# Third window's dilated pairs with v stationary, later token blocks of 256 and 320, and another model of VectorE beside GpSimd in the list schedule

## The chip, the cores and the metric

One core of one Trainium2 chip. The metric is device time in microseconds (us) of one execution; of several runs the median counts. Engines are TensorE (PE, with its weight loads PEld), VectorE (DVE), ScalarE (ACT), GpSimd (POOL) and SyncE (SP), which issues most DMAs.

## The reference

```python
# q, k, v: (4, 8, 576, 64); heads 0-3: window of 32; heads 4-7: dilated, 32 keys at a step of 4
scores = where(mask, q @ k.T / 8, -1e9)
attn = exp(scores - max(scores)); attn /= sum(attn) + 1e-9
x = (attn @ v) as (2304 tokens, 512)
h = x @ w_in;  x = maximum(0.01 * h, h) @ w_out                       # first MLP, 512 -> 2048 -> 512
h = x @ w_in2; out = (maximum(h, 0) + log1p(exp(-abs(h)))) @ w_out2   # second MLP
```

## The kernel before, in words

The 2304 tokens are cut in two ways. For attention there are eight **windows** w of 288 tokens (half a sequence each), and in each of them four **pairs** p of heads: p = 0, 1 are plain, p = 2, 3 dilated. For the first MLP there are **blocks** of tokens (`widths`, L448), and each block runs over 16 pieces f of the hidden size. One (block, f) is a **slot**. In a slot TensorE runs twelve matmuls `h<-xh,w` / `h<-xl,w` (g1, L833) and, two slots later, twelve `yp<-gh,w` / `yp<-gl,w` (g2, L876); between them ScalarE copies h out of PSUM (`hc`, L849) and rounds it (`gh`, L854), and VectorE takes the rest (`gl`, g1_lo, L858). Every operand is split into a high and a low part, so each product is three matmuls. Blocks 0 and 1 are done together, f by f, as slots 0 to 31; block 2 is slots 32 to 47, block 3 slots 48 to 63, and so on to slot 127. A block's x lies in a room of one of two buffers (`x0`, `x1`, in turn by unit; a unit is a block, blocks 0 and 1 together being unit 0), so attention for one block runs beside the slots of the block before it, and its small matmuls stand between the slots on TensorE.

A pair of attention goes: transposes of k and q (trans_k, trans_q), scores (`sc`, L661 or L674), mask (L682, L689), the maximum over keys with a PARTITION_ALL_REDUCE on GpSimd (`mx<-s`, L699), less_max (L703), exp on ScalarE, and then one of two ways. **Not turned**: pv (L724) has the probabilities stationary and v, with a column of ones for the sum, moving; ScalarE and VectorE divide (inv, L740, L741); xT (L750) transposes on TensorE; x_hi (L807) and x_lo (L811) split x. **Turned**: pv_late (L760) has v stationary, so that its result needs no transpose; the sum over keys is a second PARTITION_ALL_REDUCE (`sm<-s`, L768); VectorE spreads it (L776), inverts it (recip, L781 to L784) and multiplies (norm, L788). Windows 0 and 1 (`early`) have code of their own. Before, window 2 is not turned at all, of window 3 pairs 0, 2 and 3 are, from window 4 on all are.

Beside all this the weights of both MLPs are converted from their 64-bit form by ScalarE and VectorE (cp, cf, w: L326, L330, L339, L366, L381), and those of the second one stored in HBM as sums. From about 500 us on the second MLP runs (L1017, L1078, L1090), which the change leaves alone.

The order of every engine is found while the kernel is built: `run_schedule` (L108) is a list scheduler. Each `Op` has a cost, a due time worked back from its users' targets, slots that it acquires and releases, and the engines take the most urgent op that is ready. The order that results is fixed: on the chip each engine runs its own instructions in that order, and semaphores hold one that comes too early. For VectorE beside a reduce of GpSimd the scheduler has a model: before, an op with `lock` set runs at a share of its speed (0.33, or 0.7 for the transposes and recip) as long as the reduce lasts.

Of the kernel before, what the change touches and what calls it, by code (L numbers as in the profile page):

```python
# [11 lines left out]
F32 = mybir.dt.float32  # L12
# [14 lines left out]
def kernel(  # L27
# [22 lines left out]
    P = 128  # L50
# [4 lines left out]
    TG = 384  # L55
# [30 lines left out]
    TURN = 3  # L86
# [7 lines left out]
    class Op:  # L94
        def __init__(self, eng, cost, fn, *args, deps=(), order=(), acq=(), rel=(),
                     target=None, margin=0.0, start=0.0, lib=None, slack=0.0, lock=0.0, optional=False, hold=0.0, lead=None, shy=False):
# [11 lines left out]
    def run_schedule(slots):  # L108
# [64 lines left out]
        running = {}  # L173

        def slowed(start, work, rate):
            beside = locked - start
            return start + (work / rate if work <= rate * beside else beside + work - rate * beside)

# [5 lines left out]
        while True:  # L184
# [17 lines left out]
            for e in engines:  # L202
# [3 lines left out]
                for o in pools[e]:  # L206
                    if ready_at[o] <= now + 1e-9 and all(free[a] >= o.acq.count(a) for a in o.acq):
                        rank = (ready_at[o] if e == "bw" else o.prio) + (HOLD if switch(o) else 0.0) + (WAIT if 0.0 < o.lock < 0.5 and now < locked else 0.0), o.n
                        if best is None or rank < best_rank:
                            best, best_rank = o, rank  # L210
# [24 lines left out]
                if best.lib == "reduce":  # L235
                    locked = best.end if now > LOCK_FROM else now + LOCKED
                    beside = running.get("dve")
                    if now > LOCK_FROM and beside is not None and beside.lock and beside.end > now:
                        beside.end = slowed(now, beside.end - now, beside.lock)
                        busy["dve"] = beside.end - TRAIL["dve"]  # L240
                        heapq.heappush(events, beside.end)
                        heapq.heappush(events, busy["dve"])
# [205 lines left out]
    widths = [256, 256, 352, 288, 288, 288, 288, 288]  # L448
# [22 lines left out]

    xparts, rows = {}, {}
# [12 lines left out]
    class Pair:  # L485
        def __init__(self, w, p):
# [8 lines left out]
            self.turned = w >= TURN and (self.dil or p == 0 or w > TURN)  # L495
# [294 lines left out]
        def x_views(self):  # L790

            w0 = self.w * T1
            for u in range(NUNIT):
# [3 lines left out]
                xh, xl = (t[:, self.p, lo - unit_at[u]:hi - unit_at[u]] for t in x_room(u))  # L797
# [5 lines left out]
                yield src, xh, xl  # L803

        def x_hi(self):
            for src, hi, _ in self.x_views():
                nc.scalar.activation(out=hi, in_=src, func=AF.Copy)  # L807

        def x_lo(self):
            for src, hi, lo in self.x_views():  # L810
                nc.vector.tensor_sub(out=lo, in0=src, in1=hi.bitcast(F32))  # L811
# [326 lines left out]
    NSPIN, LOCKED, LOCK, LOCK_FROM, SLACK0, SLACK, HOLDS = 150, 1.2, 0.33, 75.0, 0.3, 1.0, 1.5  # L1138
    LOCKT = 0.7
# [53 lines left out]
    for w in range(NW):  # L1193
        blocks = [b for b, (t, n) in enumerate(BLOCKS) if t < (w + 1) * T1 and t + n > w * T1]
        first_slot = min(slot(b) for b in blocks)
        rooms = sorted({unit_of[b] for b in blocks if BLOCKS[b][0] >= w * T1 and b != 1})
        for p in range(NPAIR):
# [58 lines left out]
            else:  # L1256
                nk = a.s0 + T1 - a.klo
                tk = Op("dve", dve(nk) if not dil or a.first else 2 * dve(nk), a.trans_k, deps=[lk] + old_kq, rel=["kr"], lock=LOCKT, **m)
                tq = [Op("dve", (1.0 if turned else 1.2) if dil else 0.48, a.trans_q, deps=[lq] + (old_kq if dil else []),
                         rel=["qr"] if dil else [], lock=LOCKT, **m)]  # L1260
# [25 lines left out]
            x = Op("dve", dve(576), a.less_max, deps=[r], rel=[tag_mx], lock=LOCK, **m)  # L1286
            a.o_less = x
            x = [Op("act", act(576), a.exp, deps=[x], **m)]
            if turned:
# [3 lines left out]
                t = Op("dve", 2 * dve(288), a.spread, deps=[sm, pv], rel=[tag_mx, tag_s], lock=LOCKT, **m)  # L1293
                t = Op("dve", 0.9, a.recip, deps=[t], acq=["rd"], rel=["rd"], lock=LOCKT, **m)
# [17 lines left out]
            xh = a.o_xh = Op("act", act(288, not turned), a.x_hi, deps=[xt], order=[prev(1, "o_xh")],  # L1312
# [316 lines left out]
```

## Time and profile before

| | |
|---|---|
| median of 3 runs (lowest to highest) | 892.06 us (892.01 to 892.25) |
| profiled execution, own time | 890.93 us |
| its span | 889.1 us |
| PE busy | 878.9 us, 99% |
| PEld busy | 822.2 us, 92% |
| DVE busy | 654.1 us, 74% |
| ACT busy | 399.1 us, 45% |
| POOL busy | 146.8 us, 17%, all of it before 450 us |

The span is what the instructions of the profiled execution cover; 1.8 us lie around it. Starts in the trace count from the span's start. The end of a matmul is modelled and overlaps the next one, so what one matmul costs in a stream is read from start to start. Where a chain of waits lists "PE h L833 x12", twelve matmuls of one line are one piece, and its length is already from start to start.

### The profile page before, as it was taken

What the parts mean: (1) busy time and instruction counts of PE and PEld (TensorE: products, weight loads), DVE (VectorE), ACT (ScalarE), POOL (GpSimd) and SP (SyncE); (2) the same over time, 40 slices, a digit from 0 to 9 for tenths busy, and PEclk for the clock granted to TensorE, in tenths of its full rate; (3) what the DMA queues carried; (4) which work ended last, traced back from release to release, by engine and by line L of the source; (5) the groups of instructions that cost most, each with busy time, mean ns of one, the idle gap of its engine ahead of it and who ended that gap; (6) DMA issues with size and microseconds to landing.
All of it is one profiled execution on the core that took longest, in us unless ns stands there. A gap on an engine that the chain in (4) does not pass through costs nothing.

```text
span 889.1 us, 16856 instructions
## 1 busy us (share of the span) xinstructions
PE 878.9 (99%) x6621; PEld 822.2 (92%) x6621; DVE 654.1 (74%) x1166; ACT 399.1 (45%) x780; POOL 146.8 (17%) x71
## 2 busy tenths in 40 slices
PE   9989999999999999999999999999999999999998
PEld 6889999999999999999999999989888898888886
DVE  5999986897897887978944766857765775576553
ACT  5878765345444443444445644324322432243231
POOL 6500120332452433435400000000000000000000
PEclk9999999999999999999999999999999999999999
DMA  9887235664644626435259578333533443334332
GB/s 236 240 261 261 49 83 190 173 180 144 168 123 135 167 65 181 99 107 153 77 167 304 149 227 252 116 101 114 163 122 97 142 146 109 102 112 149 95 95 96
DMA packets 150736, 132.19 MB, mean 149 GB/s; under 512 B 92480, under 2 KB 131200, under 8 KB 150656
## 3 DMA queue, kind: packets, MB, share of 16 engines
q1 hardware_dynamic: 149632, 129.96, 49.1%
q10 hardware_dynamic: 1024, 1.15, 0.5%
q8 instruction: 52, 0.85, 0.4%
q14 instruction: 28, 0.23, 0.1%
HBM read 104.86 MB, written 26.21 MB: 147 GB/s over the span
## 4 chain that ended last, share of the span: by engine, by line
PE 94%; DMA 2%; DVE 2%; ACT 1%; issue 1%; SPq 0%; DVEq 0%; ACTq 0%
PE yp L876 23%; PE yo L1090 23%; PE h L833 23%; PE h L1017 18%; PE hp L1078 3%; DMA raw<-in_moe_w_out_dram 2%; PE pv L760 1%; PE sc L661 1%; PE sc L674 1%; PE pv L724 1%; DVE cf L330 0%; DVE w L381 0%; PE xt L750 0%; DVE cf L339 0%; DVE xn L741 0%
## 5 line engine op out<-in xcount | busy, mean ns | idle before, releaser
L876 PE MATMUL yp<-gh,w 128*128 128x288 f32 (+2 forms) x1024 | 229.1, 299 | 0.0
L833 PE MATMUL h<-xh,w 128*128 128x288 f32 (+2 forms) x1024 | 226.7, 297 | 0.0
L1090 PE MATMUL yo<-wo,w 128*128 128x512 f32 x864 | 222.8, 395 | 0.0
L1017 PEld LDWEIGHTS h<-tr,w 128*128 128x128 f32 x1344 | 174.3, 188 | 11.1
L1090 PEld LDWEIGHTS yo<-wo,w 128*128 128x128 f32 x864 | 152.5, 188 | 27.1
L1017 PE MATMUL h<-tr,w 128*128 128x256 f32 x1344 | 176.7, 279 | 0.0
L876 PEld LDWEIGHTS yp<-gh,w 128*128 128x128 f32 x1024 | 171.3, 188 | 1.9
L833 PEld LDWEIGHTS h<-xh,w 128*128 128x128 f32 x1024 | 171.1, 188 | 1.1
L833 PE MATMUL h<-xl,w 128*128 128x288 f32 (+2 forms) x512 | 151.2, 295 | 0.4 <-DVE xl L811 0.4
L876 PE MATMUL yp<-gl,w 128*128 128x288 f32 (+2 forms) x512 | 150.9, 295 | 0.0
L1055 ACT ACTIVATE ex<-ex 128x512 f32<-128x512 f32 x72 | 45.5, 632 | 159.9 <-DVE ex L1052 158.4
L849 ACT ACTIVATE hc<-h 128x288 f32<-128x288 f32 (+2 forms) x128 | 52.0, 406 | 118.2 <-PE h L833 112.5
L833 PEld LDWEIGHTS h<-xl,w 128*128 128x128 f32 x512 | 96.2, 188 | 0.9 <-DVE xl L811 0.9
L876 PEld LDWEIGHTS yp<-gl,w 128*128 128x128 f32 x512 | 96.2, 188 | 0.1
L858 DVE TENSOR_TENSOR gl<-hc,gh 128x288 fp32r<-128x288 f32 (+2 forms) x128 | 73.9, 578 | 28.7 <-ACT gh L854 27.8
L699 POOL PARTITION_ALL_REDUCE mx<-s x24 | 50.0, 2083 | 243.1 <-DVE s L682 186.8
L768 POOL PARTITION_ALL_REDUCE sm<-s x19 | 71.1, 3740 | 31.8 <-ACT s L706 27.5
L1058 DVE SCALAR_TENSOR_TENSOR ex<-hs,ex 128x512 f32<-128x512 f32 x64 | 44.3, 692 | 35.9 <-ACT ex L1055 35.6
L1063 ACT ACTIVATE w<-ex 128x512 fp32r<-128x512 f32 x72 | 45.3, 629 | 32.8 <-DVE ex L1058 32.8
L321 ACT ACTIVATE cf<-raw 128x512 f32<-128x512 f32 (+1 forms) x48 | 39.9, 830 | 40.7 <-DMA raw<-in_moe_w_out_dram 15.4
L854 ACT ACTIVATE gh<-hc 128x288 fp32r<-128x288 f32 (+2 forms) x128 | 56.6, 442 | 2.9
L1067 DVE TENSOR_TENSOR w<-ex,w 128x512 fp32r<-128x512 f32 x72 | 49.7, 691 | 10.9 <-ACT w L1063 6.2
(113 smaller groups left out, 966.6 us busy)
## 6 DMA issues: line engine op xcount, KB each, us to landing
wo<-w2o SPq DMA_DIRECT2D x80, 512.0 KB, 3.6
raw<-in_moe_w_in_dram SPq DMA_DIRECT2D x32, 512.0 KB, 6.5
raw<-in_moe_w_out_dram SPq DMA_DIRECT2D x32, 512.0 KB, 4.2
w2o<-cf SPq DMA_DIRECT2D x16, 512.0 KB, 3.1
w2a<-cf SPq DMA_DIRECT2D x8, 512.0 KB, 2.6
w2s<-cs SPq DMA_DIRECT2D x8, 512.0 KB
w<-w2a SPq DMA_DIRECT2D x8, 512.0 KB
out_dram<-o SPq DMA_DIRECT2D x28, 128.0 KB, 3.0
```

The costliest lines, as they stand in the source:

```text
L699: nc.gpsimd.partition_all_reduce(self.mx, self.sf, channels=P, reduce_op=bass_isa.ReduceOp.max)
L768: nc.gpsimd.partition_all_reduce(self.sm, self.sf, channels=P, reduce_op=bass_isa.ReduceOp.add)
L833: nc.tensor.matmul(out=h, lhsT=a[:, c, :], rhs=b_[:, c, :], start=(c == 0 and a is whi and b_ is xh), stop=(c == NC - 1 and a is wlo))
L849: nc.scalar.activation(out=hc, in_=hbank.pop(s), func=AF.Prelu, alpha=0.01)
L854: nc.scalar.activation(out=gh, in_=hcopy[s], func=AF.Copy)
L858: eng.tensor_sub(out=gl, in0=hcopy.pop(s), in1=gparts[s][0].bitcast(F32))
L876: nc.tensor.matmul(out=ybank[e][:, o:o + n], lhsT=a[:, e * P:(e + 1) * P], rhs=b_, start=(f == 0 and n == unit_len[u] and a is whi and b_ ...
L1017: nc.tensor.matmul(out=bank[m, b][:, half], lhsT=w[:, a, kb * P:(kb + 1) * P], rhs=t[:, b_, kb], start=(kb == 0 and a + b_ == 0), stop=(kb ...
L1055: nc.scalar.activation(out=self.ex, in_=self.ex, func=AF.Softplus)
L1063: nc.scalar.activation(out=self.gh, in_=self.ex, func=AF.Copy)
L1067: nc.vector.tensor_sub(out=self.gl, in0=self.ex, in1=self.gh.bitcast(F32))
L1090: nc.tensor.matmul(out=obank[c, t], lhsT=a, rhs=b_, start=(opens and n == 0), stop=(closes and n == 2))
```

## The change

Three parts.

- `TURN` goes from 3 to 2, and the condition loses its exception: window 2's dilated pairs (2 and 3) and window 3's pair 1 become turned. Window 2's plain pairs stay as they are.
- Blocks 4 to 7 are 256, 320, 256 and 320 tokens in place of 288 each. Their edges no longer fall on those of windows 4 and 6: the last 32 tokens of these windows belong to a block whose room is still in use. x_hi writes them into a buffer of their own (`x_held`), and one copy on ScalarE and one subtraction on VectorE (`hold_hi`, `hold_low`) move them on when the room is free.
- The scheduler's model: a reduce holds VectorE's ops that have `lock` for a phase from its start (1.2 for a maximum, 2.45 for a sum), and such an op then takes its whole cost behind that phase. Transposes no longer count as held, recip does.

```diff
-    TG = 384
+    TG = 352
...
-    TURN = 3
+    TURN = 2
...
                 if best.lib == "reduce":
-                    locked = best.end if now > LOCK_FROM else now + LOCKED
-                    beside = running.get("dve")
-                    if now > LOCK_FROM and beside is not None and beside.lock and beside.end > now:
...
+                    locked = now + (LOCKED if best.cost < 3.0 else LOCKEDS)
                 if best.lock and now < locked:
-                    best.end = slowed(now, best.cost, best.lock) if now > LOCK_FROM else locked + best.cost
-                running[e] = best
+                    best.end = locked + best.cost
...
-    widths = [256, 256, 352, 288, 288, 288, 288, 288]
+    widths = [256, 256, 352, 288, 256, 320, 256, 320]
...
+    split_unit = {
+        w: u for w in range(NEARLY, NW) for u in range(NUNIT) if w * T1 < unit_at[u] < w * T1 + T1}
+    HELD = T1 - widths[-2]
+    x_held = attp.tile([P, NC, HELD], F32, tag="hold", name="hold") if split_unit else None
...
-            self.turned = w >= TURN and (self.dil or p == 0 or w > TURN)
+            self.turned = w >= TURN and (self.dil or w > TURN)
...
+                held = split_unit.get(self.w) == u
+                if held:
+                    xh = xl = x_held[:, self.p, 0:hi - lo]
...
+    def hold_hi(w):
+        u = split_unit[w]
+        nc.scalar.activation(out=x_room(u)[0][:, :, 0:HELD], in_=x_held, func=AF.Copy)
+
+    def hold_low(w):
+        xh, xl = (t[:, :, 0:HELD] for t in x_room(split_unit[w]))
+        nc.vector.tensor_sub(out=xl, in0=x_held, in1=xh.bitcast(F32))
...
-    NSPIN, LOCKED, LOCK, LOCK_FROM, SLACK0, SLACK, HOLDS = 150, 1.2, 0.33, 75.0, 0.3, 1.0, 1.5
-    LOCKT = 0.7
+    NSPIN, LOCKED, LOCKEDS, SLACK0, SLACK, HOLDS = 150, 1.2, 2.45, 0.3, 1.0, 1.5
...
-                t = Op("dve", 0.9, a.recip, deps=[t], acq=["rd"], rel=["rd"], lock=LOCKT, **m)
+                t = Op("dve", 0.9, a.recip, deps=[t], acq=["rd"], rel=["rd"], lock=True, **m)
...
+                held_op = Op("act", act(NC * HELD), hold_hi, w, deps=[b_.o_xh for b_ in pairs[-NPAIR + 1:]] + [xh],
+                             acq=[f"x{u % 2}"], **m)
+                held_lo = Op("dve", dve(NC * HELD), hold_low, w, deps=[held_op], target=tau(slot(u + 1)) - 1.0, **m)
```

The new cost model also moves work: from about 95 us to 500 us the order of every engine differs. TensorE's order before that is the same, and so is that of TensorE in the second MLP.

TensorE, window 2's pair 3, its product with v, before (`v_96` is the v of odd pairs; 72x65 is one residue of the dilated window by 64 columns and the sum):

```order
L833 MATMUL h<-xl,w 128x256
L833 MATMUL h<-xh,w 128x256 x2
L833 MATMUL h<-xl,w 128x256
L833 MATMUL h<-xh,w 128x256
L724 MATMUL pv<-v_96,s 72x65 x8
L876 MATMUL yp_794<-gh,w 128x256
```

and of the change (line numbers are those of the changed kernel; L837 is g1, L880 g2, L751 pv_late):

```order
L880 MATMUL yp_849<-gh,w 128x256
L880 MATMUL yp_849<-gl,w 128x256
L880 MATMUL yp_849<-gh,w 128x256
L751 MATMUL pv<-s,v_96 64x72 x8
L837 MATMUL h<-xh,w 128x256
L837 MATMUL h<-xl,w 128x256
```

The eight products have v stationary now, and the four transposes `xt<-ident,xn 128x72` of this pair, which stood a slot later, are gone.

VectorE, the end of the same pair, before (`xt` is xT's result in PSUM):

```order
L858 TENSOR_TENSOR gl<-hc,gh 128x256 x2
L740 RECIPROCAL rd<-rd 72x4
L741 TENSOR_TENSOR xn<-pv,rd 72x256
L740 RECIPROCAL rd<-rd 72x4
L741 TENSOR_TENSOR xn<-pv,rd 72x256
L326 TENSOR_SCALAR cp<-cf 128x512
L330 SCALAR_TENSOR_TENSOR cf<-cf,cp 128x512
L339 ISA cf<-raw,cf 128x1024
L858 TENSOR_TENSOR gl<-hc,gh 128x256
L811 TENSOR_TENSOR xl<-xt,xh 128x288
```

and of the change (L862 is gl, L767 spread, L772 to L775 recip, L779 norm, L807 x_lo):

```order
L862 TENSOR_TENSOR gl<-hc,gh 128x256 x2
L767 STREAM_TRANSPOSE xn<-sm 64x288 x2
L313 TENSOR_SCALAR cp<-cf 128x512
L772 TENSOR_SCALAR rd<-xn 128x9
L774 RECIPROCAL rd<-rd 128x9
L775 STREAM_TRANSPOSE xn<-rd 128x288
L317 SCALAR_TENSOR_TENSOR cf<-cf,cp 128x512
L779 TENSOR_TENSOR xn<-pv,xn 128x288
L862 TENSOR_TENSOR gl<-hc,gh 128x256
L326 ISA cf<-raw,cf 128x1024
L807 TENSOR_TENSOR xl<-xn,xh 128x288
```

Four divisions became two transposes, three steps of recip and norm, with the first of them behind GpSimd's sum; the last x_lo stands behind the same gl, that of slot 28, as before.

VectorE, the end of window 4, before:

```order
L788 TENSOR_TENSOR xn<-pv,xn 128x288
L339 ISA cf<-raw,cf 128x1024
L811 TENSOR_TENSOR xl<-xn,xh 128x288
L858 TENSOR_TENSOR gl<-hc,gh 128x288
L326 TENSOR_SCALAR cp<-cf 128x512
L330 SCALAR_TENSOR_TENSOR cf<-cf,cp 128x512
L858 TENSOR_TENSOR gl<-hc,gh 128x288
```

and of the change (L815 is hold_low):

```order
L779 TENSOR_TENSOR xn<-pv,xn 128x288
L862 TENSOR_TENSOR gl<-hc,gh 128x288
L317 SCALAR_TENSOR_TENSOR cf<-cf,cp 128x512
L807 TENSOR_TENSOR xl<-xn,xh 128x256
L326 ISA cf<-raw,cf 128x1024
L862 TENSOR_TENSOR gl<-hc,gh 128x288
L673 TENSOR_TENSOR s<-sc,masksb 128x3x96 x2
L594 STREAM_TRANSPOSE kt_93<-kr 128x104x4
L815 TENSOR_TENSOR xl<-hold,xh 128x4x32
L862 TENSOR_TENSOR gl<-hc,gh 128x288
```

The last x_lo of window 4 stood behind the gl of slot 62 and stands behind that of slot 61 now; hold_low waits until g1 of slot 63 has left its room, and is ahead of that slot's gl.

## Rows read from the trace of the kernel before

**Rows 1.** The page's first part: busy us, share of the span, instructions.

```profile
PE 878.9 (99%) x6621; PEld 822.2 (92%) x6621; DVE 654.1 (74%) x1166; ACT 399.1 (45%) x780; POOL 146.8 (17%) x71
```

**Rows 2.** Busy time by stretch: length, each engine's busy us, PEclk, DMA.

```profile
100.00:146.00 46.00, 46.00 (x417) 45.60 (x416) 37.69 (x72) 26.97 (x55) 7.07 (x3) 1.00 0.39 98
146.00:214.00 68.00, 68.00 (x483) 66.41 (x483) 56.57 (x101) 32.74 (x65) 19.44 (x7) 1.00 0.62 180
...
60.00:495.00 435.00, 435.00 (x3510) 426.52 (x3508) 352.36 (x621) 218.88 (x439) 121.06 (x43) 1.00 0.52 152
```

**Rows 3.** The chain of waits: start, us, twelve matmuls of 256, 352, 288.

```profile
86.05 1.40 PE h L833 x12
...
152.87 1.92 PE h L833 x12
...
249.62 1.60 PE h L833 x12
```

**Rows 4.** Timeline of TensorE, window 2's pair 2: pv, then xT.

```profile
119.72 0.28 PE L876 MATMUL yp<-gh,w 128*128 128x256 f32 x1
...
121.04 0.28 PE L833 MATMUL h<-xl,w 128*128 128x256 f32 x1
...
126.03 0.28 PE L833 MATMUL h<-xh,w 128*128 128x256 f32 x1
...
126.57 0.28 PE L876 MATMUL yp<-gl,w 128*128 128x256 f32 x1
```

**Rows 5.** The same, a turned dilated pair of window 4: pv_late.

```profile
266.31 0.29 PE L876 MATMUL yp<-gh,w 128*128 128x288 f32 x1
...
267.41 0.30 PE L833 MATMUL h<-xl,w 128*128 128x288 f32 x1
```

**Rows 6.** The same, plain pairs: pv of window 2, pv_late of window 5.

```profile
96.61 0.28 PE L833 MATMUL h<-xh,w 128*128 128x256 f32 x1
...
97.89 0.28 PE L876 MATMUL yp<-gl,w 128*128 128x256 f32 x1
...
301.50 0.29 PE L833 MATMUL h<-xh,w 128*128 128x288 f32 x1
...
302.60 0.29 PE L876 MATMUL yp<-gl,w 128*128 128x288 f32 x1
```

**Rows 7.** VectorE's groups by form: busy us, mean ns of one, idle before.

```profile
L776 DVE STREAM_TRANSPOSE xn<-sm 64x288 f32<-64x288 f32 x38 | 17.8, 468 | 2.4 <-POOL sm L768 2.2
L784 DVE STREAM_TRANSPOSE xn<-rd 128x288 f32<-128x288 f32 x19 | 9.1, 478 | 0.6
L788 DVE TENSOR_TENSOR xn<-pv,xn 128x288 f32<-128x288 f32 x19 | 8.5, 448 | 0.3
L741 DVE TENSOR_TENSOR xn<-pv,rd 72x256 f32<-72x256 f32 x12 | 5.1, 421 | 1.2
L740 DVE RECIPROCAL rd<-rd 72x4 f32<-72x4 f32 x12 | 2.0, 166 | 0.7 <-ACT rd L734 0.7
```

**Rows 8.** Timeline of GpSimd, VectorE and TensorE around two sums of window 5.

```profile
308.74 3.59 POOL L768 PARTITION_ALL_REDUCE sm<-s  x1 [1.60 <-ACT s L706]
...
309.02 2.57 DVE L811 TENSOR_TENSOR xl<-xn,xh 128x288 fp32r<-128x288 f32 x1
...
320.18 3.61 POOL L768 PARTITION_ALL_REDUCE sm<-s  x1 [1.60 <-ACT s L706]
...
320.26 2.78 DVE L858 TENSOR_TENSOR gl<-hc,gh 128x288 fp32r<-128x288 f32 x1
322.96 0.71 DVE L811 TENSOR_TENSOR xl<-xn,xh 128x288 fp32r<-128x288 f32 x1
...
324.47 0.30 PE L876 MATMUL yp<-gl,w 128*128 128x288 f32 x1
```

**Rows 9.** The same: window 5's last x_lo, and its block's first matmul.

```profile
328.99 0.71 DVE L811 TENSOR_TENSOR xl<-xn,xh 128x288 fp32r<-128x288 f32 x1 [0.81 <-ACT xh L807]
...
332.37 0.29 PE L833 MATMUL h<-xh,w 128*128 128x288 f32 x1
```

More of the change, by code (lines that the diff above doesn't have):

```diff
@@ L171, in begins @@
                 coming[u.eng].append(u)
[L173 to L177, printed above, removed]
         result = []
@@ L207, in run_schedule @@
                     if ready_at[o] <= now + 1e-9 and all(free[a] >= o.acq.count(a) for a in o.acq):
[L208 removed]
+                        rank = (ready_at[o] if e == "bw" else o.prio) + (HOLD if switch(o) else 0.0) + (WAIT if o.lock and now < locked else 0.0), o.n
                         if best is None or rank < best_rank:
@@ L802, in x_views @@
                     src = self.xp.rearrange("p i m -> p (i m)")[:, lo - w0:hi - w0]
-                yield src, xh, xl
+                yield src, xh, xl, held
         def x_hi(self):
-            for src, hi, _ in self.x_views():
+            for src, hi, _, held in self.x_views():
                 nc.scalar.activation(out=hi, in_=src, func=AF.Copy)
         def x_lo(self):
-            for src, hi, lo in self.x_views():
-                nc.vector.tensor_sub(out=lo, in0=src, in1=hi.bitcast(F32))
+            for src, hi, lo, held in self.x_views():
+                if not held:
+                    nc.vector.tensor_sub(out=lo, in0=src, in1=hi.bitcast(F32))
+    def hold_hi(w):
[4 more added lines that the diff above has]
+        nc.vector.tensor_sub(out=xl, in0=x_held, in1=xh.bitcast(F32))
     gparts = {}
@@ L1195 @@
         first_slot = min(slot(b) for b in blocks)
-        rooms = sorted({unit_of[b] for b in blocks if BLOCKS[b][0] >= w * T1 and b != 1})
+        rooms = sorted({unit_of[b] for b in blocks if BLOCKS[b][0] >= w * T1 and b != 1 and split_unit.get(w) != unit_of[b]})
         for p in range(NPAIR):
@@ L1311 @@
                 a.o_xt = xt
-            xh = a.o_xh = Op("act", act(288, not turned), a.x_hi, deps=[xt], order=[prev(1, "o_xh")],
+            xh = a.o_xh = Op("act", act(288, not turned) + (0.2 if w in split_unit else 0.0), a.x_hi, deps=[xt], order=[prev(1, "o_xh")],
                              acq=[] if not turned else room, **m)
             stag = STAG00 if w == 0 else STAG0 if w == 1 else STAG
-            xl = Op("dve", dve(288, not turned), a.x_lo, deps=[xh], rel=[a.room(p)[1] if not turned else "xn"], lock=LOCK if turned else 0.0,
+            xl = Op("dve", dve(288, not turned), a.x_lo, deps=[xh], rel=[a.room(p)[1] if not turned else "xn"], lock=turned,
                     target=tau(first_slot) - 0.5 - stag * (NPAIR - 1 - p), **m)
@@ L1318 @@
                 xready.setdefault(b, []).append(xl)
+            if p == 0 and w - 1 in split_unit:
+                xh.order.append(held_op)
+            if p == 0 and w - 2 in split_unit:
+                xh.order.append(held_lo)
+            if p == NPAIR - 1 and w in split_unit:
+                u = split_unit[w]
+                held_op = Op("act", act(NC * HELD), hold_hi, w, deps=[b_.o_xh for b_ in pairs[-NPAIR + 1:]] + [xh],
+                             acq=[f"x{u % 2}"], **m)
+                held_lo = Op("dve", dve(NC * HELD), hold_low, w, deps=[held_op], target=tau(slot(u + 1)) - 1.0, **m)
+                xready.setdefault(u + 1, []).append(held_lo)
             last_att.append(xl)
```

31 lines of the change are left out of this document (14 added, 17 removed).

## The prediction, made before the changed kernel ran

> **What bounds the kernel now.** I read the page's first part first: TensorE is busy for 99% of the span, the next engine, VectorE, for 74% [rows 1]. A share of busy time can hide waits, because the ends of matmuls are modelled, so I looked at stretches next. [...] Whatever the change takes from TensorE's work comes off the time, as long as no other engine makes TensorE wait; whatever it adds to the others is free until it does.
>
> All durations are from the profiled execution, whose own time is 890.93 us; the median of the runs shown is 1.13 us above it. I sum differences and set them against the median, 892.06. About 0.2% of it, 1.8 us, is what a measurement of this kernel can tell from no change; so faster means under 890.28, slower over 893.84.
>
> **The widths.** Blocks 4 to 7 are 32 pieces of twelve matmuls each (16 slots, g1 and g2). Before, 128 pieces of 288; now 64 of 256 and 64 of 320. The columns are the same, 64 x 576. A piece of 256 costs 1.40 us. No piece of 320 is in the trace; the nearest rows are 288 and 352, 1.60 and 1.92, and between them a line gives 1.76 for 320 [rows 3]. [...] The sum is 64 x (2 x 1.60 - 1.40 - 1.76) = **2.6 us less**, with 0 and 3.5 as its ends (3.5 for 1.745).
>
> [...]
>
> **Three pairs turned, on TensorE.** I take each step from start to start, over the matmul before and the first one behind it, and subtract what the two cost in a stream. pv of a dilated pair that is not turned: 119.72 to 121.04 is 1.32, less 2 x 0.117, 1.09; xT: 126.03 to 126.57, less the same, 0.31 [rows 4]. pv_late: 266.31 to 267.41 is 1.10, less 2 x 0.133, 0.83 [rows 5]. So a dilated pair saves 0.57. A plain pair: 96.61 to 97.89 less 0.23 is 1.05, pv_late 301.50 to 302.60 less 0.27 is 0.83 [rows 6], and for its xT I take the 0.31 of the dilated one; it saves 0.53. Two dilated and one plain: **1.7 us less**. Ends: 1.5 and 1.9, for reading starts to 0.02 us.
>
> **What the three pairs add elsewhere.** VectorE gets two spreading transposes (0.47 each), one transpose of recip (0.48), norm (0.45) and two small steps, for which I take 0.17 each, and loses two reciprocals of 0.17 and two products of 0.42 [rows 7]: 2.2 in place of 1.2, so 1.0 more per pair. GpSimd gets a sum of 3.6 us per pair. What such a sum does to VectorE is in the timeline: an x_lo that began 0.28 us behind the start of a sum took 2.57 us, a gl 0.08 behind one took 2.78, an x_lo 2.78 behind one 0.71 [rows 8]. Unheld, an operation on the same 128x288 took 0.45 [rows 7]. So an operation is held until about 2.4 us from the sum's start, at most 2.3 us of loss, and not later. Per pair that is between 1.0 and 3.4 us more for VectorE, for three pairs 3 to 10. Two of the pairs lie in 100 to 146 us, where VectorE is idle for 8.3 of 46 us, the third in 146 to 214, with 11.4 idle; GpSimd works 7 and 19 us there [rows 2]. So it fits, and it is not on the path: gl is needed two slots after its g1. Even the gl that was held for 2.78 us ended at 323.04 and was first read by a matmul at 324.47 [rows 8]. Behind a spread that waits for its sum, gl of the next slot is queued, and behind that TensorE's g2; that is the place to look if it goes wrong. I cost this at nothing, with 0 to 2 us for the range. It cannot gain, since TensorE has no idle time there to give back.
>
> **The held tokens.** For two windows, four more small copies on ScalarE, hold_hi there and hold_low on VectorE. ScalarE is idle half of the time [rows 2]. hold_low waits for the g1 of slot 63 and stands ahead of that slot's gl, which needs the same g1, so it delays it by its own length, below the 0.45 of a 288-wide operation [rows 7]. Nothing. The DMAs are as many as before, SP issues some loads of k, q, v and weights in another order, and none of these is on the chain after 60 us. Nothing, with the pace of attention (second rival) as the risk.
>
> **The scheduler's model.** It removes no instruction. The rows agree better with the new one: held until a phase has passed, then the whole cost, rather than a slower pace as long as the sum lasts; the x_lo of 322.96 was finished before its sum was [rows 8]. With no idle time on TensorE in this stretch a better order can bring nothing by itself; a worse one can cost.
>
> **Sum.** 2.6 + 1.7 = 4.2 us (4.23 unrounded). The profiled execution would go from 890.93 to 886.7, the median from 892.06 to **887.8 us**.
>
> **The rivals.**
> 1. The widths bring nothing, because 320 carries more than 288 does (1.80 a piece). Then only the pairs count: 892.06 - 1.7 = 890.4. For it: no row of 320. [...] Chance 0.11.
> 2. Attention comes too late for a narrower block. Block 4 is 32 x 0.20 = 6.4 us shorter now, so window 5 is needed that much sooner. Before, its last x_lo ended at 329.70, and its block began at 332.37 [rows 9]: 2.7 us to spare. At the old pace TensorE would wait 3.7 us: 891.5. Against it: in VectorE's order that x_lo now stands behind the gl of slot 76 instead of 77, the block's first slot being 80, and that of window 4 behind 61 instead of 62. The wider block gives the next window its time back. Chance 0.08.
> 3. Slower: VectorE's queue overflows in the slots of 100 to 214 us. There windows 2 and 3 get the three new sums while the weights of the first MLP and of the second are being converted. The price is what doesn't fit: up to 3 x 3.4 = 10 us, 898 at worst. It decides from 6.0 us on, 4.2 of gain and 1.8 of bound. For it: conversions were moved ahead, in front of the attention of window 2. Against it: 20 us of idle time in the two stretches. Chance 0.06, at 894 to 898.
> 4. A sum holds VectorE to its end, 3.6 us and not 2.4, so that the new order, planned with 2.45, runs 1.2 us late at each of 22 sums; if all of it reached TensorE, 22 x 1.2 = 26 us, 914. Against it stand the operations that ended before their sum did [rows 8]. [...] Chance 0.02.
>
> **How the numbers follow.** The forecast keeps 0.73. It is under 890.28 whole, and so is a small part of the first rival: faster 0.75. The rest of the first and the second: same 0.17. The third and fourth: slower 0.08. The range reaches down to 886.6, for 320 at its lower bound (1.0 less) and 0.2 of the pairs, and up to 891.8, over both "same" rivals and the 2 us that VectorE may cost. It leaves out the last two rivals and some of the forecast's edges.
>
> **What would show it.** Right: in the changed profile pieces of twelve at 256 take 1.40 us and at 320 take 1.76; no idle time on TensorE from 60 us to the second MLP; the last g2 about 4 us earlier; pv_late for window 2's dilated pairs at 0.83. VectorE busier between 100 and 214 us, and GpSimd with 22 sums of 3.6 us. Wrong: 320 at 1.80; idle time on TensorE ahead of `h<-xl` at the start of block 5 or 7 (second rival); idle time ahead of `yp<-gl` around window 2's or 3's sums (third); gl operations that last 3.6 us and more beside a sum (fourth).

## The result, and the profile after

The change made the kernel slower: 896.49 us median of 4 runs (895.48 to 897.05) beside 892.03 us for the kernel before, ratio 1.0051, 95% interval 1.0034 to 1.0069. Forecast was 887.8 us with a range to 891.8, and 0.08 for slower. The profiled execution took 897.05 us, its span is 895.3 us. Each run further down was measured in turn with the kernel before, whose median was 890.96 to 891.31 us there; a ratio is to that median, with its 95% interval in brackets.

The page's first part of the changed kernel, against [rows 1], and the busy time by stretch, against [rows 2] (length, each engine's busy us, granted clock, DMA share, GB/s):

```profile
PE 879.9 (98%) x6610; PEld 820.5 (92%) x6610; DVE 662.9 (74%) x1176; ACT 398.7 (45%) x785; POOL 158.9 (18%) x74
```

```profile
100.00:146.00 46.00, 44.84 (x398) 43.45 (x398) 42.35 (x69) 25.43 (x51) 16.38 (x5) 1.00 0.34 81
146.00:214.00 68.00, 68.00 (x487) 66.09 (x487) 58.01 (x102) 30.33 (x61) 22.94 (x8) 1.00 0.59 169
214.00:276.00 62.00, 59.12 (x468) 56.59 (x467) 54.42 (x100) 29.24 (x65) 23.60 (x8) 1.00 0.55 157
...
60.00:495.00 435.00, 430.15 (x3468) 418.84 (x3467) 356.59 (x623) 214.86 (x437) 133.80 (x46) 1.00 0.51 149
```

TensorE has idle time in the first MLP now, 4.85 us of 435 where there was none. Almost all of it is in two places, 100 to 146 us (1.16) and 214 to 332 us (3.65), and none in 146 to 214. The clock is 1.00 throughout, so this is waiting and not a slower engine. The idle time is a lower bound, because ends of matmuls are modelled. So I measured stretches from the first g1 matmul of one slot to that of a later one, in each trace (one execution each). "The last g2" is the start of the first matmul of slot 127's g2, so that last piece, 0.17 us longer at 320 columns than at 288, is not in the stretch:

| kernel (profiled execution), us | slots 16 to 32 | 32 to 48 | 48 to the last g2 | span |
|---|---|---|---|---|
| before | 53.54 | 68.37 | 293.64 | 889.1 |
| after | 54.81 | 67.97 | 298.05 | 895.3 |
| m_model_only | 54.97 | 69.00 | 295.29 | 892.7 |
| t_turn_only | 52.99 | 72.32 | 294.18 | 894.8 |
| w_widths_only | 53.65 | 68.45 | 293.32 | 888.7 |
| tw_old_model | 52.84 | 71.05 | 293.92 | 892.5 |
| x_store | 54.82 | 67.97 | 293.56 | 889.5 |
| x_load | 54.82 | 67.97 | 292.12 | 887.6 |
| x_both | 54.80 | 67.97 | 292.12 | 888.3 |
| y_stray | 54.17 | 67.95 | 293.48 | 888.5 |
| y_stray4 | 53.79 | 67.95 | 294.38 | 889.4 |
| y_m | 54.97 | 68.37 | 293.62 | 892.8 |
| y_mw | 54.99 | 68.45 | 292.18 | 889.3 |
| y_tw | 53.45 | 67.94 | 294.60 | 890.7 |
| y_w | 53.82 | 68.89 | 293.37 | 890.0 |
| z_phase | 54.77 | 67.95 | 295.45 | 891.8 |
| v_hybrid | 52.47 | 68.31 | 296.56 | 896.9 |
| v_hybrid3 | 54.19 | 68.32 | 295.61 | 896.5 |
| v_hybridb | 53.41 | 67.95 | 294.44 | 889.3 |
| v_hybrid3b | 54.20 | 67.97 | 294.57 | 889.7 |

From the start of the last g2 to the end it is 380.4 to 381.5 us in all of them. What comes before slot 16 moves by some 3 us between these executions (92.0 to 95.0; v_hybrid and v_hybrid3, whose start has another order, 98.1 and 96.9). The changed kernel's execution has 0.8 us more of it than that of before. So the span of a single execution says less than its stretches.

**The rows that went as forecast.** The chain of waits in block 5 (320 wide) of the changed kernel, and TensorE's timeline around pv_late of window 2's pair, against [rows 3] and [rows 4, 5]:

```profile
345.20 1.76 PE h L837 x12
346.96 1.77 PE yp L880 x12
```

```profile
135.29 0.28 PE L880 MATMUL yp<-gh,w 128*128 128x256 f32 x1
135.50 0.72 PE L751 MATMUL pv<-s,v 104*64 104x72 f32 x16
136.16 0.40 PE L837 MATMUL h<-xh,w 128*128 128x256 f32 x1
136.39 0.28 PE L837 MATMUL h<-xl,w 128*128 128x256 f32 x1
```

A piece of 320 takes 1.76 us, as taken. The pair turned: 135.29 to 136.39 less two matmuls of 0.117 is 0.87 us, where 0.83 had been taken and pv with xT had 1.40, so such a pair saves 0.53 and not 0.57. In slots 32 to 48, where the plain pair is turned and nothing waits, the stretch is 0.4 us shorter (0.53 had been taken).

**The rows that did not.** The chain of waits in block 3 of the changed kernel. Before, the chain of this stretch was pieces of matmuls throughout; now no matmul stands in it from 220.74 to 238.30 us:

```profile
222.14 2.18 DMA qr<-in_q_dram
...
225.14 0.60 DVE cf L326
...
227.03 0.60 DVE cf L353
227.63 0.21 DVE ys L898
...
230.41 6.32 DMA raw<-in_moe_w_out_dram
...
236.75 0.68 ACT cf L308
...
237.45 0.03 DVE cp L313
...
237.79 0.46 DVE xn L779
...
238.30 0.91 PE sc L665 x10
```

Why a load of the second MLP's weights (`raw`) ends up ahead of attention's scores is in the timelines. SyncE, ScalarE and VectorE of the changed kernel (start, us, engine and line, operation; in brackets the idle time before and what ended it):

```profile
228.10 2.26 SPq L901 DMA_DIRECT2D y<-ys  x4
230.41 0.48 SPq L296 DMA_DIRECT2D raw<-in_moe_w_out_dram  x1
```

```profile
217.39 0.68 ACT L308 ACTIVATE cf<-raw 128x512 f32<-128x512 f32 x1 [2.01 <-DMA w2o<-cf]
...
222.05 0.66 ACT L308 ACTIVATE cf<-raw 128x512 f32<-128x512 f32 x1 [1.77 <-DMA w2a<-cf]
...
236.75 0.67 ACT L308 ACTIVATE cf<-raw 128x512 f32<-128x512 f32 x1 [2.79 <-DMA raw<-in_moe_w_out_dram]
```

```profile
223.26 0.43 DVE L313 TENSOR_SCALAR cp<-cf 128x512 uint32<-128x512 uint32 x1 [2.49 <-DMA w2s<-cs]
...
235.31 0.48 DVE L775 STREAM_TRANSPOSE xn<-rd 128x288 f32<-128x288 f32 x1
237.45 0.43 DVE L313 TENSOR_SCALAR cp<-cf 128x512 uint32<-128x512 uint32 x1 [1.66 <-ACT cf L308]
237.79 0.45 DVE L779 TENSOR_TENSOR xn<-pv,xn 128x288 f32<-128x288 f32 x1
```

Read from the last row back: the last input of norm (`xn<-pv,xn`) was ready at 235.79, when recip's transpose ended, but norm stands behind `cp` in VectorE's order and began at 237.79. `cp` needs ScalarE's `cf`, and ScalarE stands still for 2.79 us until 512 KB of weights land that SyncE issued at 230.41. At 217 and 222 us it is the other end of the same conversion: ScalarE's `cf` waited 2.01 and 1.77 us there until the store that read its buffer (`w2o`, `w2a`) had landed. VectorE kept its order in these rows, with norm beginning 0.34 us behind the start of `cp`, 2.0 us after its input was ready; so the load for which ScalarE stood still 2.79 us held attention too, up to the scores at 238.30. The load came late for two reasons that this chain doesn't separate: it was issued behind other work in SyncE's order (a store of converted weights and four of `y`, which waited for VectorE), and it took 6.32 us to land, where the median of such loads between 60 and 495 us is 5.0 (4.2 before).

The longest single wait in TensorE's timeline is of another kind, on the copies of block 2's result out of PSUM (`ys`) on ScalarE:

```profile
227.11 0.40 PE L880 MATMUL yp<-gh,w 128*128 128x288 f32 x1 [1.09 <-ACT ys L896]
```

### The profile page after: what moved, and what is told of

It reads as the page before. It is cut to its first block, busy times and chain, and to the rows that moved or that the text cites. A ratio compares the mean times of both kernels' runs of the same rounds, so it can differ in the third digit from the quotient of the medians.

```text
span 895.3 us, 16850 instructions
## 1 busy us (share of the span) xinstructions
PE 879.9 (98%) x6610; PEld 820.5 (92%) x6610; DVE 662.9 (74%) x1176; ACT 398.7 (45%) x785; POOL 158.9 (18%) x74
## 4 chain that ended last, share of the span: by engine, by line
PE 84%; DMA 7%; DVE 4%; ACT 2%; issue 1%; SPq 1%; DVEq 0%; ACTq 0%
PE yo L1094 22%; PE yp L880 18%; PE h L837 18%; PE h L1021 18%; DMA raw<-in_moe_w_out_dram 5%; PE hp L1082 3%; DMA lent<-in_v_dram 2%; PE pv L751 1%; PE sc L652 1%; PE sc L665 1%; ACT cf L308 1%; PE pv L715 1%; DVE w L368 1%; SPq L533 1%; DVE cf L326 1%
## 5 line engine op out<-in xcount | busy, mean ns | idle before, releaser
L880 PE MATMUL yp<-gh,w 128*128 128x256 f32 (+3 forms) x1024 | 229.7, 299 | 1.9 <-ACT ys L896 1.1
L837 PE MATMUL h<-xh,w 128*128 128x256 f32 (+3 forms) x1024 | 226.4, 297 | 0.0
L880 PEld LDWEIGHTS yp<-gh,w 128*128 128x128 f32 x1024 | 172.1, 188 | 5.0 <-DVE ys L898 1.6
L837 PEld LDWEIGHTS h<-xh,w 128*128 128x128 f32 x1024 | 171.1, 188 | 1.4
L880 PE MATMUL yp<-gl,w 128*128 128x256 f32 (+3 forms) x512 | 151.2, 295 | 0.3 <-DVE gl L862 0.3
L837 PE MATMUL h<-xl,w 128*128 128x256 f32 (+3 forms) x512 | 150.9, 295 | 0.4 <-DVE xl L807 0.4
L862 DVE TENSOR_TENSOR gl<-hc,gh 128x256 fp32r<-128x256 f32 (+3 forms) x128 | 79.7, 624 | 31.1 <-ACT gh L858 30.5
L837 PEld LDWEIGHTS h<-xl,w 128*128 128x128 f32 x512 | 96.3, 188 | 0.9 <-DVE xl L807 0.9
L880 PEld LDWEIGHTS yp<-gl,w 128*128 128x128 f32 x512 | 96.3, 188 | 0.7 <-DVE gl L862 0.5
L853 ACT ACTIVATE hc<-h 128x256 f32<-128x256 f32 (+3 forms) x128 | 51.8, 404 | 100.1 <-PE h L837 85.2
L690 POOL PARTITION_ALL_REDUCE mx<-s x24 | 53.1, 2212 | 218.7 <-DVE s L673 182.4
L759 POOL PARTITION_ALL_REDUCE sm<-s x22 | 80.7, 3668 | 45.6 <-ACT s L697 45.6
L308 ACT ACTIVATE cf<-raw 128x512 f32<-128x512 f32 (+1 forms) x48 | 39.9, 831 | 40.8 <-DMA raw<-in_moe_w_out_dram 15.1
L858 ACT ACTIVATE gh<-hc 128x256 fp32r<-128x256 f32 (+3 forms) x128 | 56.7, 443 | 3.0
```

The lines of the kernel that those rows point to most:

```text
L308: nc.scalar.activation(out=self.cff, in_=self.raw[:, :, 1].bitcast(F32), func=AF.Copy, scale=2.0 ** -112)
L690: nc.gpsimd.partition_all_reduce(self.mx, self.sf, channels=P, reduce_op=bass_isa.ReduceOp.max)
L759: nc.gpsimd.partition_all_reduce(self.sm, self.sf, channels=P, reduce_op=bass_isa.ReduceOp.add)
L837: nc.tensor.matmul(out=h, lhsT=a[:, c, :], rhs=b_[:, c, :], start=(c == 0 and a is whi and b_ is xh), stop=(c == NC - 1 and a is wlo))
L853: nc.scalar.activation(out=hc, in_=hbank.pop(s), func=AF.Prelu, alpha=0.01)
L858: nc.scalar.activation(out=gh, in_=hcopy[s], func=AF.Copy)
```

## The experiments

Two theories at first: the extra waits come from the new model's orders as such, or from what the turned pairs and widths crowd onto VectorE.

**The parts one by one.** Four kernels: the change's third part alone; `TURN` and its condition alone; the widths with the held tokens alone; the last two together.

```diff
 m_model_only:    -locked = best.end if now > LOCK_FROM else now + LOCKED
                +locked = now + (LOCKED if best.cost < 3.0 else LOCKEDS)
 t_turn_only:     -TURN = 3
                +TURN = 2
 w_widths_only:   -widths = [256, 256, 352, 288, 288, 288, 288, 288]
                +widths = [256, 256, 352, 288, 256, 320, 256, 320]
 tw_old_model:  the last two
```

> The kernel before with the new scheduler model alone; every instruction is that of before, only the order differs. In the changed kernel TensorE did 4.2 us less work, yet the time rose by 4.5, so some 9 to 10 us of waiting came in. Theory 1 (the model makes an order that waits): all of it is here, 900 to 902 us. Theory 2 (the added pairs and the narrower blocks crowd the other queues, the model is harmless): 891.5 to 892.5. Theory 3 (any new order costs some luck): between, 893 to 897.

> The kernel before with the three pairs turned, old model, old widths. The work on TensorE is 1.7 us less. Theory 1: 890.4. Theory 2: the sums and the VectorE steps of the three pairs take their share of the loss, 893 to 897, with waits on TensorE between 95 and 215 us. Theory 3: 890 to 895.

> The kernel before with blocks of 256, 320, 256, 320 and the held tokens, old model, old pairs. The work on TensorE is 2.6 us less (64 pieces of 1.40 and 64 of 1.76 for 128 of 1.60). Theory 1: 889.5. Theory 2: narrower blocks make attention late or the queues crowded, 891 to 896, with waits at the start of blocks 5 and 7. Theory 3: 889 to 894.

> The changed kernel with the old scheduler model. The work on TensorE is that of the changed kernel, 4.2 us less than before. Theory 1: 887.8, the time that was forecast for the change. Theory 2: 896, as the changed kernel. Theory 3: anything from 888 to 896.

Measured: model alone 895.85 us, ratio 1.0057 (1.0037 to 1.0077), though not one matmul differs; pairs alone 894.42, 1.0032 (1.0020 to 1.0044); widths alone 891.39, 1.0006 (0.9994 to 1.0018); pairs and widths 893.70, 1.0022 (1.0011 to 1.0032). All four lie in the ranges of theory 3 (any new order costs some luck), t_turn_only and w_widths_only in those of theory 2 too. No part gave what its work promised. The waits lie in different places, though: with the model alone in slots 16 to 32 (1.4 us) and behind slot 48 (1.7), with turned pairs and the old model in slots 32 to 48. So "the model" and "the crowding" are both incomplete: each of these orders has waits of its own. The chain of the model alone in block 3 shows the same mechanism as the change, with another load:

```profile
235.57 5.31 DMA raw<-in_moe_w_in_dram
...
240.90 0.69 ACT cf L308
...
241.61 0.44 DVE cp L313
```

With turned pairs and the old model it is one wait of 2.1 us on gl, held beside a sum. The old model plans a third of the pace there, for the 0.53 us of this gl about 1.6, and it took 2.85; that this is why it was put there is not shown. With the slower matmuls behind it (last section) that makes 3.3 of the 4.4 us by which slots 32 to 48 exceed the 67.97 of the kernels with the same pair turned and no wait. Timeline of VectorE and GpSimd of t_turn_only, and the stretches around it (the columns as above; the eighth value is the clock):

```profile
205.33 3.61 POOL L768 PARTITION_ALL_REDUCE sm<-s  x1 [1.60 <-ACT s L706]
205.40 2.85 DVE L858 TENSOR_TENSOR gl<-hc,gh 128x352 fp32r<-128x352 f32 x1
```

```profile
206.00:208.40 2.40, 0.33 (x3) 0.10 (x1) 2.40 (x2) 0.06 (x1) 2.40 (x1) 1.00 0.55 218
208.40:212.00 3.60, 3.60 (x17) 3.22 (x19) 3.36 (x8) 1.95 (x4) 0.54 (x1) 0.53 0.00 0
```

**The late transfers taken away, order unchanged.** Three kernels whose instructions on TensorE, VectorE, ScalarE and GpSimd stand in the change's order, one by one; SyncE lacks the loads in two of them.

```diff
 x_store (w2a, w2s and w2o alike):
-            nc.sync.dma_start(out=d, in_=self.ct.bitcast(F32).rearrange("p (t n) -> p t n", t=2))
+            nc.sync.dma_start(out=d, in_=wparts[NF - 1, 0].bitcast(F32))
 x_load (in the load; the conversion reads a tile of weights that is there):
+            if self.layer:
+                return
 x_both: the two together
```

> The changed kernel, every engine's order the same; only the stores of the second layer's converted weights (w2o, w2a, w2s) read a finished tile of the first layer's weights instead of what was just converted, so no conversion waits for a store to free its buffer, and SyncE waits for no conversion. Left out: the second MLP gets wrong weights. Theory 1 (transfers of the second layer's weights that land later than planned hold the head of ScalarE's and VectorE's queues, and TensorE waits behind them): 889 to 893. Theory 2 (VectorE's queue itself is too full where sums hold it): 895 to 897, as the changed kernel.

> The changed kernel, every engine's order the same, without the loads of the second layer's weights: the conversion reads a finished tile of the first layer's weights. So no conversion waits for a load; the stores stay. Left out: the second MLP gets wrong weights, and 16.8 MB of loads are gone. Theory 1: 890 to 894, less than the stores and this together. Theory 2: 895 to 897.

> Both of these at once, every engine's order the same: the conversions of the second layer run, but wait for no transfer. Left out: the second MLP gets wrong weights, 16.8 MB of loads are gone. Theory 1: TensorE waits nowhere from 100 us on, 887 to 889, the forecast for the change. Theory 2: 895 to 897, with the same waits on TensorE as in the changed kernel.

Measured: 891.77 (ratio 1.0009, 0.9999 to 1.0018) without the wait for stores, as theory 1 had it; **889.84** (0.9987, 0.9977 to 0.9996) without the loads, just below theory 1's 890 to 894, and more than the stores gave, not less; 890.10 (0.9982, 0.9967 to 0.9997) without either, above its 887 to 889 and no better than without the loads alone. Theory 2 (895 to 897) is out in all three. The waits in slots 16 to 32 stayed, and the widths give less than forecast (below); so the forecast's time did not come back. The chain of x_load in the stretch that held the waits is matmuls again:

```profile
228.62 1.80 PE yp L887 x12
230.41 1.60 PE h L844 x12
232.01 1.58 PE yp L887 x12
233.59 0.84 PE sc L672 x12
```

From slot 48 on, 298.05 us became 293.56 and 292.12. So 5.9 us of the changed kernel go when nothing has to wait for these transfers; widths, pairs, copies and the order are all still there. x_load also lowers the DMA traffic, from a share of 0.51 to 0.39 between 60 and 495 us; x_store does not (0.52), and takes 4.5 of the 5.9. Each also frees SyncE of some of its waits for conversions, before a store or before the next load; which link of that ring (load, conversion, store, the next load) costs how much was not taken apart. The two effects overlap: without the loads, taking the stores' wait away too gives nothing more.

**The late transfers planned for.** If lateness is the cause, an order that expects it should do. The scheduler has a constant for that, used for the start only:

```diff
-    STRAY, STRAY_FROM, STRAY_TO = 2.5, 14.0, 45.0
+    STRAY, STRAY_FROM, STRAY_TO = 2.5, 14.0, 480.0
```

> The changed kernel with one number of the scheduler changed: a landing transfer counts 2.5 us more until 480 us, not only from 14 to 45 us, so the conversions are planned behind later landings. Nothing is left out. Theory 1: 888 to 892. Theory 2: 894 to 897, a new order with the same trouble.

Measured 890.12 us, ratio 0.9991 (0.9982 to 1.0001), with all of the work: 0.6% below the change by the ratios to the kernel before, and about 1 us faster than before, which the interval can't quite tell from none. It lies in theory 1's range. ScalarE still waits 1.00 us for a raw load at 232 us there, but no wait on TensorE follows from it. Behind slot 48 it takes 293.48 us, 1.4 more than x_load, so 4.6 of the 5.9 us went. (Waits behind slot 48 are counted this way from here on: the stretch less that of x_load, or less that of before for a kernel with the old widths.)

The same with parts of the change:

> The change without its pairs turned (widths and scheduler's model), and the order planned with landings 2.5 us later than the model's own in the whole first MLP. Landings theory: the waits for second-layer weights are gone, so it gives 892 less the 2.6 us of the widths plus little: 889 to 890.5; and since the three new sums of windows 2 and 3 are away, the waits on TensorE at 99 to 137 us fall below 1 us. Rival (the scheduler's model makes bad orders whatever the landings): 891 to 896.

> Pairs and widths with the old scheduler's model, and the later landings in the plan. Landings theory alone: 887.8 to 890 (it was 893.7 without the later landings). Rival (the old model places gl where a sum holds it, one wait of about 2 us at 204.6 us, which no later landing cures): 891 to 893.

> The kernel before with the new scheduler's model alone, and the later landings in the plan. TensorE's work is that of the kernel before. Landings theory: 891 to 892.5, the time of the kernel before (it was 895.9 without the later landings). Rival (the new model itself costs): 894 to 896.

> The kernel before with the widths alone and the later landings in the plan, old scheduler's model. Sum by measured pieces (256 at 1.417 us, 288 at 1.602, 320 at 1.763): 1.55 us less than before, 889.5, if no wait is added; with the waits that the widths alone showed (its time was 891.4), 891.

Model and widths: 891.42 (1.0003, 0.9993 to 1.0013), above the 889 to 890.5 that the theory gave and in the rival's range. Behind slot 48 it did as expected, 292.18 us against 293.62 of the model alone, with no waits left. But slots 16 to 32 kept their 55.0 us, without a turned pair; that expectation fell. Pairs and widths: 891.81 (1.0011, 1.0002 to 1.0021), in the rival's range, though not by its mechanism: the wait at 205 us, which was none for a transfer, is gone, and 2.5 us of others stand behind slot 48, where tw_old_model had 1.8. Model alone: 892.15 (1.0015, 1.0005 to 1.0024) in place of 895.85, as expected. Widths alone: 892.43 (1.0011, 1.0003 to 1.0020), no better than without the later landings (891.39), a miss: it has 1.3 us of waits behind slot 48, where w_widths_only had 1.2, and 0.4 in slots 32 to 48.

**Chance or rule.** The change with one number of its model moved, and the change with 4.0 us for landings in place of 2.5:

```diff
 z_phase:   -LOCKEDS = 2.45
            +LOCKEDS = 2.6
 y_stray4:  -(STRAY if o.eng == "bw" and STRAY_FROM < o.end < STRAY_TO else 0.0)
            +((STRAY if o.end < 45.0 else 4.0) if o.eng == "bw" and STRAY_FROM < o.end < STRAY_TO else 0.0)
```

> The change whole, with one number of its scheduler's model moved: the phase of a sum is 2.60 us in place of 2.45, so the order is a slightly different one; the work is the same. Landings theory (nothing in the plan allows for late landings): 893 to 897, like the change. Rival (the loss is the luck of one order): it may fall anywhere between 889 and 897, and below 891 speaks for luck.

> The change with landings planned 4.0 us later than the model's own behind 45 us, in place of 2.5 (890.1). Landings theory: the waits left in slots 48 to 64 (one of 0.65 us at 254.8 us) go: 889 to 890. Rival (a new order, new waits): 890.5 to 893. The 2 us of waits in window 2 stay in either case.

z_phase: 893.16 (1.0024, 1.0015 to 1.0034), at the low end of the landings theory's range, which lies within the rival's; its waits behind slot 48 are 3.3 us where the change has 5.9. y_stray4: 890.82 (0.9995, 0.9986 to 1.0003), the rival's range: the wait at 254.8 us did not go but grew, to one of 1.5 us on norm. So what the late transfers cost is in part the luck of an order: 3.3 to 5.9 us for one number of the plan. Planning for later landings is no rule either: behind slot 48 it took the waits from 5.9 us to 1.4 and from 1.7 to none in the two orders of the new model, but from 1.8 to 2.5 and from 1.2 to 1.3 in those of the old one, and 4.0 us of it did worse than 2.5.

**Window 2.** What is left is 2.2 us in slots 16 to 32 of the change and of x_load, 1.5 in y_stray: the stretch against that of before, less the 1.1 us that the two turned pairs should give and the 0.2 us that g2 grew by (below). Of the 2.2 us the profile shows 1.16 as idle time on TensorE. VectorE's timeline at the first plain pair of window 2, before:

```profile
109.36 1.19 DVE L330 SCALAR_TENSOR_TENSOR cf<-cf,cp 128x1024 uint32<-128x1024 uint32 x1
110.47 0.41 DVE L858 TENSOR_TENSOR gl<-hc,gh 128x256 fp32r<-128x256 f32 x1
110.80 0.17 DVE L740 RECIPROCAL rd<-rd 96x6 f32<-96x6 f32 x1
111.07 0.55 DVE L741 TENSOR_TENSOR xn<-pv,rd 96x384 f32<-96x384 f32 x1
```

and after:

```profile
111.46 1.19 DVE L317 SCALAR_TENSOR_TENSOR cf<-cf,cp 128x1024 uint32<-128x1024 uint32 x1
112.75 0.69 DVE L313 TENSOR_SCALAR cp<-cf 128x1024 uint32<-128x1024 uint32 x1
113.36 0.42 DVE L862 TENSOR_TENSOR gl<-hc,gh 128x256 fp32r<-128x256 f32 x1
113.70 1.22 DVE L326 CUSTOM_DVE_ANT_0 cf<-raw,cf 128x2048 uint16<-128x2048 uint16 x1
114.83 0.18 DVE L731 RECIPROCAL rd<-rd 96x6 f32<-96x6 f32 x1
115.11 0.55 DVE L732 TENSOR_TENSOR xn<-pv,rd 96x384 f32<-96x384 f32 x1
```

```profile
115.81 0.73 PE L652 MATMUL sc<-qz,kt 128*128 128x144 f32 x4 [0.28 <-DVE xn L732]
```

Two conversions (0.69 and 1.22 us) now stand between `cf` and `rd`. From the start of `cf` to that of `xn` it is 3.65 us, it was 1.71, and TensorE's scores wait for `xn`; the other wait that the profile shows here, 0.43 us at 103.62, is on VectorE's mask (L673). To see whether the model or the turned pairs do this, two kernels with the old model until 146 us of the plan and the new one behind it (but for recip, which is not held there), with and without window 2's pairs turned, both with the widths and the later landings. A first form of both also moved the order of the start:

```diff
-                    locked = best.end if now > LOCK_FROM else now + LOCKED
+                    locked = best.end if LOCK_FROM < now < LOCK_TO else now + (LOCKED if best.cost < 3.0 else LOCKEDS)
...
-                    best.end = slowed(now, best.cost, best.lock) if now > LOCK_FROM else locked + best.cost
+                    best.end = slowed(now, best.cost, best.lock) if now < LOCK_TO else locked + best.cost
 v_hybrid3, besides:
-            self.turned = w >= TURN and (self.dil or w > TURN)
+            self.turned = w > TURN
```

> Widths and pairs turned, later landings in the plan, and the scheduler's model split in time: the old one until 146 us, so for window 2, the new one behind it. Theory that the new model's order puts the conversions of weights ahead of window 2's attention (1.4 us of waits, there with or without turned pairs) and that the turned pairs cost 1.0 us more of waits there: slots 16 to 32 take 53.4 us in place of 54.2, behind them 0 to 1.5 us of waits, 888.7 to 889.9, faster than before (891). Rival (any new order brings its own new waits of 1 us and more): 890 to 891.5.

> The same, but window 2's two dilated pairs are not turned, only the plain pair of window 3. Theory (the two pairs give 1.1 us and their waits in window 2 take 1.0 back): the same time as with them within 0.4 us, 888.7 to 890, and slots 16 to 32 at 53.5 us as in the kernel before. Rival (the turned pairs cost more in waits than they give): 1 us and more faster than with them.

897.55 (1.0067, 1.0054 to 1.0079) and 898.41 (1.0079, 1.0065 to 1.0092): slots 0 to 16 took 57.8 and 57.2 us in place of 53.4, so the totals, outside both ranges, answer another question. Behind slot 48 they have 4.4 and 3.5 us of waits too, with later landings in the plan. Slots 16 to 32, which they were made for, took 52.47 and 54.19. The second form keeps the start as it was (`LOCK_FROM < now < LOCK_TO` in the last line too, `LOCKEDS` only behind `LOCK_TO`):

> The split model again, with the order before 75 us left as it was (the first split had also moved the start, slots 0 to 16 took 57.8 us in place of 53.5). The order until 146 us is that of the old model with turned pairs: slots 16 to 32 take 53.4 us. Theory: the waits behind it are those of late landings and are planned for, 0 to 1.5 us: 889 to 890.3. Rival (each new order has a new wait somewhere): 890.5 to 892.

> As before, without the two turned pairs of window 2. If these pairs give 1.1 us and cost about 1.0 in waits: 53.5 us for slots 16 to 32, and the same time as with them within 0.5 us. If orders differ by luck, more than 1 us from it, either way.

891.36 (1.0003, 0.9994 to 1.0012) and 892.19 (1.0013, 1.0004 to 1.0022). v_hybridb has 53.41 us in slots 16 to 32, as expected, and 2.3 us of waits behind slot 48: the rival's range. Without the turned pairs the stretch takes 54.20 us where 53.5 was expected, 0.8 longer than with them, and the time is 0.8 us longer, neither "the same within 0.5" nor "more than 1". So between these two orders the turned pairs bring 0.8 of their 1.1 us in window 2. Kernels with the new model have 53.8 to 55.0 us there, those with the old one 52.5 to 53.8 with the pairs turned or as before (v_hybrid3 and v_hybrid3b 54.2): more of the waits seem to belong to the model's order than to the pairs (the model alone and model with widths have 54.97 and 54.99 there without a turned pair in window 2), but the groups overlap, and the shares stay open.

## Why the prediction was wrong

- **TensorE's work: right in sign, 1.5 us too large.** The pairs' 1.7 us nearly held: 0.53 for a dilated pair by its rows and 0.4 for the plain one in slots 32 to 48 make 1.5 (between v_hybrid3b and v_hybridb the two dilated ones gave 0.8, some of it beside waits). The widths' 2.6 us were mis-sized. Start to start over all matmuls of one width that follow one of the same line (from 276 us on, without those over 12 ns from the median), 288 takes 133.4 ns in g1 and 133.5 in g2, 320 takes 146.5 and 147.3, but 256 takes 117.8 and 118.3. The 1.40 us of [rows 3] for a piece of 256 were those of blocks 0 and 1 (117.0 and 117.1); in blocks 4 and 6 it is 1.42. So blocks 4 to 7 should be 1.5 us shorter: y_mw against y_m shows 292.18 against 293.62, and x_load against before 292.12 against 293.64, 1.4 and 1.5; with the last piece, which these stretches leave out, 1.3 and 1.4. And in blocks 0 and 1, where no width changed, g2 went from 117.1 to 118.3 ns in w_widths_only and in the change, 0.2 us in each 16 slots (m_model_only and t_turn_only have 117.0 and 117.2). In all about 1.1 us in place of 2.6. The mis-sized term is the piece of 256, its 1.40 taken from blocks 0 and 1. The ends of the forecast's 2.6, 0 and 3.5, take a piece of 320 at 1.80 and at 1.745 us, which no run shows; in the changed kernel it is 1.76 in g1 and 1.77 in g2. In these streams 32 columns more cost 15.6 ns in g1 and 15.2 in g2 from 256 to 288, and 13.1 and 13.8 from 288 to 320.
- **"SP issues some loads of k, q, v and weights in another order, and none of these is on the chain after 60 us. Nothing, with the pace of attention (second rival) as the risk"** is the step that failed, with the new order that it belongs to. That no load was on the chain was read from the old order; in the new one loads and stores of the second MLP's weights are on it, for 5.9 us behind slot 48. ScalarE's waits for loads of weights, 200 to 335 us, before, after and in x_store (us in total, times, longest):

```profile
ACT cf L321 <- DMA raw<-in_moe_w_in_dram: 5.2, 3, 2.2
ACT cf L321 <- DMA raw<-in_moe_w_out_dram: 4.6, 3, 2.9
```

```profile
ACT cf L308 <- DMA raw<-in_moe_w_out_dram: 8.3, 4, 3.9
ACT cf L308 <- DMA raw<-in_moe_w_in_dram: 4.6, 3, 2.9
```

```profile
ACT cf L308 <- DMA raw<-in_moe_w_out_dram: 11.5, 5, 4.4
ACT cf L308 <- DMA raw<-in_moe_w_in_dram: 3.6, 3, 1.5
```

  Before, 9.8 us of such waits cost TensorE nothing; after, they are 12.9 (over the whole kernel 26.0, 26.5 before), and with those for stores they cost 5.9; in x_store, whose order on both engines is the change's, 15.1 us of them go with a loss of 1.4. So the length of ScalarE's waits doesn't set the price. What does, as I read the chain, is whether the work of attention behind them still comes in time for TensorE; the runs show that for norm at 237.79, not for every wait. "With no idle time on TensorE in this stretch a better order can bring nothing by itself; a worse one can cost" (435.00 of 435.00 us busy from 60 to 495 us, [rows 2]) was right, and was given no price: the model alone, without one matmul more or less, costs 4.5 us, more than the sum of all gains forecast.
- **VectorE at nothing, with 0 to 2 us for the range**: 2.2 us of waits in slots 16 to 32 (54.81 less 53.54, plus the 1.1 that the two pairs should have given, less 0.2 for g2). The bound was about right and the place too, but for another reason than the load of the three pairs: the waits stand behind a mask and behind `rd` and `xn` of a plain pair, not behind a spread, and the model alone, with no new turned pair, has 1.4 us of them.
- **The rivals.** The second did not occur: blocks 5 and 7 began without a wait. The third had the right sign, the sentence "conversions were moved ahead, in front of the attention of window 2", and 2 of the 8 us; the rest came at 214 to 332 us, through transfers it did not speak of. The first was half true by another cause: 320 cost 1.76 as taken, but 256 cost more. The fourth is refuted again: in t_turn_only gl beside the sum of 205.33 took 2.85 us and was done 0.7 us before the sum was.

The sum as it came out, profiled executions: widths -1.5, g2 of blocks 0 and 1 in slots 16 to 32 +0.2, pairs -1.5 (1.1 and 0.4), window 2 +2.2, late transfers +5.9, the start +0.8 (with another 0.2 of g2 in it); together +6.1, spans 889.1 and 895.3. It closes because window 2 is what its stretch leaves over; the start is chance of single executions as far as these traces tell. In medians the loss is 4.5 us.

No version that does all of the work beats the kernel before by more than its interval. y_stray comes nearest and beats the change clearly; x_load shows, with work and traffic left out, that an order without these waits might be worth about 1.2 us (0.4 to 2.0 by its interval).

## What to carry to other kernels

When a change makes a scheduler lay a new order, price the new order, not only the instructions: list which transfers an engine's next instruction waits for, how late each may land, and what urgent work is behind it. ScalarE's 9.8 us of waits for loads cost TensorE nothing in the order before, and 12.9 us of them with those for stores cost 5.9 us in the next, so the busy share and even the sum of waits of an engine don't tell its price. To see whether such transfers are the cause, take their waits away with every order kept. Planning for later landings helped in two orders of four here; so compare several orders of the same work before judging an edit of 0.3% (890.1, 890.8, 893.2 and 896.5 us here).

## What was not expected of the hardware

- After TensorE had stood for 2.1 us in t_turn_only (busy 0.33 of 2.40 us), its granted clock was 0.53 over the next 3.6 us, where it was 1.00 before and behind: nine matmuls of 352 in a row took 133 ns more each, and in the chain of waits eleven took 3.48 us from 208.30 on, where twelve take 1.92 in [rows 3]. That is 1.2 us and more on top of the wait. tw_old_model had a like wait, 2.1 us on gl, and its slots 32 to 48 took 71.05 us beside the 72.32 of t_turn_only; by this difference of 1.3 us its matmuls behind the wait seem to have kept their pace, an estimate.
- The time of a 256-wide matmul is not one number: 117.0 ns in g1 of blocks 0 and 1, 117.8 in blocks 4 and 6, and in g2 of blocks 0 and 1 117.1 before, 118.3 when only the widths of later blocks and the length of gh and gl's tiles (`TG`, 384 to 352) had changed. The cause is open; neither was changed alone.
